# Per-partition running maxima, joined once, in a fused attention and soft-MoE kernel with a written-out order

## The chip, the cores and the metric

The kernel runs on one core of one Trainium2 chip. The time is device microseconds of one execution. Before the change three runs took 286.15, 287.49 and 510.6 us, so the median is 287.49; the third run is far off the other two. The profiled execution took 286.1 us, and its span, from the first to the last instruction, is 284.3 us.

## The reference

Four batches of 5056 tokens with 256 channels go through an attention over channels and then, all 20224 tokens together, through a soft mixture of experts with 32 slots (8 experts with 4 slots each). Cut to what matters:

```python
qn, kn = q / norm(q over tokens), k / norm(k over tokens)
s = kn.T @ qn / tau                    # 256 x 256 for each batch
a = softmax of s over its last axis
x = v @ a                              # tokens x 256, all batches stacked
logits = x @ phi                       # tokens x 32
d = softmax of logits over all tokens  # one column for each slot
slot_input = d.T @ x                   # 32 x 256
slot_out = relu(slot_input @ w1[e]) @ w2[e]      # expert of each slot
c = softmax of logits over the 32 slots          # one row for each token
out = c @ slot_out
```

The softmax over tokens needs for each slot a maximum over the tokens of all batches. Any value that stands for the maximum cancels, as long as sums and weights are scaled by the same one.

## The kernel before

**Tiling.** A batch is cut into ten units of 512 tokens (`UB`, a load `raw` of 1 MB with q and k) and into five pieces of 1024 tokens (`PB`, numbered p = 0 to 19, a load `v` of 1 MB). TensorE adds up S = k.T q over the units (L226), partly from fp32 data (`raw`) and partly from a split into a rounded value and a rest (`hl`, made by ScalarE at L182 and VectorE at L188). ScalarE squares each unit (L203) and VectorE adds the squares (L209) for the norms. After a batch's last unit the steps `att_*` turn S into the attention matrix a and into M = a times phi (L332), which the logits need.

**Logits.** The logits of a piece need v turned, with channels on partitions, in two halves m of 512 KB. A half is either loaded turned from HBM (`vt`; the set `LT` lists these pairs (p, m)) or turned on TensorE (`turn`, L351, eight transposes for a half) and copied by ScalarE (L356). `logits` (L378) leaves a bank of 128 partitions with four blocks of 32 slots: a partition holds one slot for a quarter of the piece's tokens. From this bank ScalarE copies the raw logits (`lt`, L399), VectorE takes a maximum (`mxs`, L405) and transposes 32x32 blocks into `nat` (L409), which has tokens on partitions.

**Groups and the running maximum.** The pieces of a batch form two groups, of three and of two pieces (`GR`). When a group's maxima are there, a chain joins the four blocks and the groups so far: `peak` (L415) on VectorE, `peak_row` (L420, a matmul that lays the 128 maxima in a row), `peak_run` (L426 to L431, maximum over the blocks and over the past), `shift` (L435, a matmul back onto partitions) and `shifted` (L440, L444: the negative maximum `negm` and the step `al` from the one before). Only then can ScalarE take the exponential (L456, in place in `lt`), VectorE transpose it to weights `dn` (L466), and `gather` on TensorE (L485) add weights times v. `finish_*` scale and add up groups and batches: a fold of the four blocks by a matmul with `fold` (L506), and a sum over batches `acc` on 32 partitions (L539). After the last batch come `last_*` (slot inputs, L547 to L575) and the experts (`up`, `relu`, `flip_h`, `back_h`, `down`, L642 to L673), whose weights are loaded into buffers that the loop has left (`load_w1`, `load_w2`).

**Output.** For each batch `c_max` to `c_mul` (L580 to L598) make the softmax over slots in `nat`, `c_flip` (L608) transposes it back, and `out_mul` (L712), `out_evict` (L734, L736) and `store` (L742, L744) write the result. Stores of the first five pieces are split into two halves of columns, because the experts' output comes in two halves.

**Order.** Every step is put in a list with a key, and the list `ORDER` of numbers says in which order the steps are emitted. Each engine runs its own part of this order strictly in sequence, and SyncE issues all DMAs in it, waiting at each for its buffer (5 buffers `raw`, 3 `hl`, 6 `v`, 3 for each `vt` half).

## Time and profile before

| what | value |
|---|---|
| median of the runs shown | 287.49 us |
| profiled execution, its own time | 286.1 us |
| its span | 284.3 us |
| TensorE busy | 248.8 us (88%) |
| VectorE busy | 236.4 us (83%) |
| ScalarE busy | 185.0 us (65%) |
| bytes moved by DMA | 115.61 MB, mean 407 GB/s |
| mean granted TensorE clock | 0.959 |

Busy time of TensorE is that of its matmuls; the loads of their weights (PEld) run beside them. The 40 slices of the page are 7.1 us each. The DMA row shows what share of the time the 16 DMA engines were moving packets, and below it how many bytes they moved. In the queries by stretch of time, each row has the stretch, then busy time and number of instructions of PE, PEld, DVE (VectorE), ACT (ScalarE) and POOL (GpSimd), then the granted clock, the DMA share and GB/s.

### The profile page before, as it was taken

To read this page: it belongs to the slowest core of one execution; us is meant where nothing else is said; L and a number is where in the kernel's file an instruction comes from. 1 tells how busy PE (TensorE), PEld (TensorE's weight loads), DVE (VectorE), ACT (ScalarE), POOL (GpSimd) and SP (SyncE) were. 2 spreads that over 40 slices of the span, in tenths; PEclk is the share of its full clock that TensorE was granted. 3 is DMA by queue.
4 is the path that set the end of the run, shared out by engine and by line. 5 is a ranking of instruction groups with operands and counts; after the bars stand their busy time and mean duration, and the time that the engine had idled before them with its cause. 6 is when DMAs were issued, how large, how long until landed. Compare 5 with 4: busy or idle time off the path is not lost. (4 is left out here: it accounts for less than half of the span.)

```text
span 284.3 us, 6083 instructions
## 1 busy us (share of the span) xinstructions
PE 248.8 (88%) x2448; PEld 201.1 (71%) x2448; DVE 236.4 (83%) x389; ACT 185.0 (65%) x264; POOL 9.8 (3%) x10
## 2 busy tenths in 40 slices
PE   6899999999999999999999999999889898984000
PEld 6699998897898978878778686786553777763000
DVE  1699999899999999999999999988768688994100
ACT  4997897889899796687777957175613436862200
POOL 0000002200003000000200000100000000000000
PEclk9999999999999999999999999999999999998555
DMA  7999999999999999999999999999999998999996
GB/s 280 428 418 420 417 421 424 422 420 414 414 422 368 399 427 422 422 407 422 415 424 421 415 418 422 418 427 417 422 413 414 414 372 323 410 423 418 426 424 260
DMA packets 19900, 115.61 MB, mean 407 GB/s; under 512 B 2336, under 2 KB 2336, under 8 KB 9248
## 3 DMA queue, kind: packets, MB, share of 16 engines
q1 hardware_dynamic: 19872, 115.22, 98.4%
q8 instruction: 19, 0.31, 0.4%
q14 instruction: 9, 0.07, 0.1%
HBM read 94.24 MB, written 20.97 MB: 405 GB/s over the span
## 5 line engine op out<-in xcount | busy, mean ns | idle before, releaser
L209 DVE TENSOR_TENSOR sq<-sq,sq 128x1024 f32<-128x1024 f32 (+1 forms) x63 | 85.2, 1366 | 1.3 <-ACT sq L203 0.6
L203 ACT ACTIVATE sq<-raw 128x2048 f32<-128x2048 f32 x40 | 76.2, 1911 | 15.2 <-DVE sq L209 6.7
L226 PE MATMUL S<-raw 128*128 128x256 f32 x328 | 80.1, 384 | 2.2 <-DMA raw<-in_qk_dram 2.2
L226 PE MATMUL S<-hl 128*128 128x256 f32 x468 | 70.9, 297 | 0.1
L226 PEld LDWEIGHTS S<-raw 128*128 128x128 f32 x328 | 58.8, 190 | 12.7 <-issue 3.3
L226 PEld LDWEIGHTS S<-hl 128*128 128x128 f32 x468 | 61.0, 190 | 3.2 <-issue 1.2
L188 DVE TENSOR_TENSOR hl<-raw,hl 128x1024 fp32r<-128x1024 f32 x39 | 46.8, 1214 | 6.9 <-ACT hl L182 6.9
L182 ACT CAST hl<-raw 128x1024 fp32r<-128x1024 f32 x39 | 40.2, 1041 | 2.6 <-PE S L226 1.7
L736 DVE COPY o<-op_None 128x512 f32<-128x512 f32 x30 | 18.7, 675 | 7.6 <-issue 6.9
L734 ACT COPY o<-op_None 128x512 f32<-128x512 f32 x30 | 15.8, 593 | 12.2 <-issue 7.9
L712 PE MATMUL op_None<-so,cT 32*128 32x256 f32 x240 | 18.6, 401 | 1.9 <-ACT o L734 1.3
L485 PE MATMUL G<-v,dn 128*32 128x256 f32 x320 | 20.1, 382 | 0.1
L712 PEld LDWEIGHTS op_None<-so,cT 32*128 32x128 f32 x240 | 14.6, 184 | 5.6 <-ACT o L734 2.7
L378 PE MATMUL L<-vt,M 128*32 128x256 f32 (+1 forms) x272 | 17.7, 380 | 0.9 <-ACT M L332 0.9
L356 ACT COPY vt<-vTp 128x512 f32<-128x512 f32 x18 | 10.4, 583 | 11.1 <-PE vTp L351 11.1
L248 POOL TENSOR_TENSOR rn<-rn,half 128x4 f32<-128x4 f32 x4 | 9.0, 2262 | 173.4 <-DVE rn L243 173.4
L485 PEld LDWEIGHTS G<-v,dn 128*32 128x32 f32 x320 | 10.0, 109 | 6.6 <-issue 0.5
L351 PE MATMUL vTp<-ident,v 128*128 128x128 f32 x96 | 14.1, 276 | 0.0
L378 PEld LDWEIGHTS L<-vt,M 128*32 128x32 f32 x272 | 8.1, 109 | 6.9 <-ACT M L332 1.3
L351 PEld LDWEIGHTS vTp<-ident,v 128*128 128x128 f32 x96 | 11.1, 143 | 2.4 <-issue 1.2
L399 ACT COPY lt<-L 128x256 f32<-128x256 f32 x20 | 7.2, 372 | 7.6 <-DVE mxs L405 3.4
L734 ACT COPY o<-op 128x256 f32<-128x256 f32 x20 | 6.3, 380 | 7.1 <-PE op L712 7.1
(111 smaller groups left out, 250.2 us busy)
## 6 DMA issues: line engine op xcount, KB each, us to landing
raw<-in_qk_dram SPq DMA_DIRECT2D x40, 1024.0 KB, 8.7
v<-in_v_dram SPq DMA_DIRECT2D x20, 1024.0 KB, 10.0
out_dram<-o SPq DMA_DIRECT2D x15, 1024.0 KB, 12.0
vt<-in_vt_dram SPq DMA_DIRECT2D x21, 512.0 KB, 8.7
w<-in_moe_w_dram SPq DMA_DIRECT2D x8, 1024.0 KB, 13.8
w<-in_moe_w_dram SPq DMA_DIRECT2D x16, 512.0 KB, 10.0
out_dram<-o SPq DMA_DIRECT2D x10, 512.0 KB, 4.3
vt<-in_vt_dram SPq DMA_DIRECT2D x4, 480.0 KB, 9.3
```

The source lines that it names most:

```text
L182: act.copy(hl[:, :ns, 0::2, :], raws[u][:, :ns])
L188: dve.tensor_tensor(hl[:, :ns, 1::2, :], raws[u][:, :ns], hl[:, :ns, 0::2, :].bitcast(F32), op=ALU.subtract)
L203: act.activation(sq, raws[u], AF.Square)
L209: dve.tensor_tensor(a[:, lo:hi], a[:, lo:hi], s[:, lo:hi], op=ALU.add)
L226: pe.matmul(sm, w, x, start=first, stop=False, skip_group_check=True)
L351: pe.transpose(tp[:, P * jj : P * jj + P], vs[p][:, 4 * h + jj, P * m : P * m + P], ident)
L356: act.copy(x[:, h * UT : h * UT + UT], tps[p, h, m])
L378: pe.matmul(L[S * g : S * g + S, :n, :], M[:, m, :], x[:, :n, S * g : S * g + S], start=m == 0, stop=m == 1,)
L485: pe.matmul(gp[S * g : S * g + S, :C], dn[:, x, j, :], vt[:, j, :], start=x == 0 and j < G, stop=x == n - 1 and j >= G,)
L712: pe.matmul(ops[b, p, hf, g][:, h, :], cT[b][S * g : S * g + S, 4 * i : 4 * i + 4, :].rearrange("s j t -> s (j t)"), so[S * g : S * g + S] ...
L734: act.copy(dst, src)
L736: dve.tensor_copy(dst, src)
```

## The change

The running maximum is no longer joined over the four blocks at each group. Each of the 128 partitions keeps its own running (negative) maximum: `logit_max` writes the negative maximum of a piece beside the running one, `peak` takes the minimum of the group's and the running one in a single reduction, and the exponentials use that as their bias. `peak_row`, `peak_run`, `shift` and `shifted` are gone. Since the four blocks of a slot now have maxima of their own, folding them is put off: for the first three batches the fold's matmul is a plain transpose (with `ident`), `acc` has 128 partitions and `gts` 128 columns. After the last group `join_*` makes one factor for each partition (a matmul, a reduction, a product, a reduction, an exponential) and puts it into the last batch's fold (`fw`), into the product that folds `acc` (`fa`) and into the sum `zacc`.

The raw logits are copied into a buffer that stays for the whole batch (`lg`); the exponentials go to a buffer of their own (`el`). `logit_nat` is now one transpose from `lg` for a whole batch, ahead of its `c_max`, and the five transposes from the PSUM banks are gone. `c_flip` writes back into `lg`, in five parts for the first batch and in two (2 and 3 pieces) for the others.

`LT` gets `- {(6, 1), (13, 1)}`. In Python a difference of sets binds more tightly than a union, so the two pairs are taken out of the last set of the expression, `{(10, 1), (13, 1), (15, 1)}`, alone; (6, 1) is still in an earlier one. The list goes from 28 turned loads to 27, and piece 13 gets two more rounds of transposes.

`ORDER` is a new list (974 steps for 1022), and the warm-up has 9 matmuls for 7.

```diff
-WAKE = 7
+WAKE = 9
+NY = 2
-LT = {(p, 0) for p in range(15)} | {(p, 1) for p in range(0, 15, 3)} | {(p, 0) for p in range(15, 20)} | {(10, 1), (13, 1), (15, 1)}
+LT = {(p, 0) for p in range(15)} | {(p, 1) for p in range(0, 15, 3)} | {(p, 0) for p in range(15, 20)} | {(10, 1), (13, 1), (15, 1)} - {(6, 1), (13, 1)}
 ORDER = [
-    1, 0, 2, 5, 3, 4, 13, 7, 8, 9, 10, 23, 6, 14, 16, 15, 31, 606, 18, 22, 17, 19, 25, 24, 21, 27, 36, 32, 41, 12,
+    615, 1, 0, 4, 2, 14, 7, 8, 12, 11, 13, 32, 9, 10, 3, 5, 18, 19, 31, 41, 16, 17, 22, 25, 26, 30, 29, 577, 21, 40,
...
     def logit_max(p):
         b, gi, x, n = group(p)
-        if x == 0:
-            mxs[b, gi] = bpool.tile([P, 3], F32, tag="mxs", name=f"mxs{b}_{gi}", bufs=2)
-        dve.tensor_reduce(mxs[b, gi][:, x : x + 1], Ls[p], axis=AX.XY, op=ALU.max)
+        m = mx_tile(b, gi)
+        dve.tensor_reduce(m[:, x + 1 : x + 2], Ls[p], axis=AX.XY, op=ALU.max, negate=True)
 
-    def logit_nat(p):
-        b, q = divmod(p, PB)
+    def logit_nat(b, q, n):
+        if b not in nat:
+            nat[b] = keep.tile([P, 8 * PB, S], F32, tag="nat", name=f"nat{b}", bufs=NY)
         dve.transpose(
-            nat[b][:, 8 * q : 8 * q + 8, :].rearrange("p j s -> p (j s)"), Ls[p].rearrange("p j s -> p (j s)")
+            nat[b][:, 8 * q : 8 * q + 8 * n, :].rearrange("p j s -> p (j s)"),
+            lg[b][:, q : q + n].rearrange("p q x -> p (q x)"),
         )
...
     def peak(b, gi):
+        m = mx_tile(b, gi)
+        negm = mx_tile(*after(b, gi))[:, 0:1]
+        lo = 1 if (b, gi) == (0, 0) else 0
+        dve.tensor_reduce(negm, m[:, lo : 1 + GR[b][gi]], axis=AX.X, op=ALU.min)
         negms[b, gi] = negm
         if (b, gi) != (0, 0):
             al = bpool.tile([P, 1], F32, tag="al", name=f"al{b}_{gi}", bufs=3)
-            dve.tensor_tensor(al, negm, run["negm"], op=ALU.subtract)
+            dve.tensor_tensor(al, negm, m[:, 0:1], op=ALU.subtract)
             als[b, gi] = al
...
+    def join_row():
+        t = bank(X1, "join")
+        pe.matmul(t[:, :P], negms[B - 1, gl].broadcast_to([P, P]), ident, start=True, stop=True)
+        run["join"] = t
+
+    def join_top():
+        top = bpool.tile([P, S], F32, tag="top", name="top")
+        dve.tensor_reduce(top, run["join"][:, :P].rearrange("p (g s) -> p s g", g=G), axis=AX.X, op=ALU.min)
+        dve.tensor_tensor(top, top, fold, op=ALU.mult)
+        jm = bpool.tile([P, 1], F32, tag="jm", name="jm")
+        dve.tensor_reduce(jm, top, axis=AX.X, op=ALU.add)
+        run["jm"] = jm
+
+    def join_exp():
+        wj = bpool.tile([P, 1], F32, tag="wj", name="wj")
+        act.activation(wj, negms[B - 1, gl], AF.Exp, bias=run["jm"], scale=-1.0)
+        run["wj"] = wj
+
+    def join_fold():
+        run["fw"] = bpool.tile([P, S], F32, tag="fw", name="fw")
+        dve.tensor_scalar_mul(run["fw"], fold, run["wj"])
+
+    def join_acc():
+        run["fa"] = bpool.tile([P, S], F32, tag="fa", name="fa")
+        dve.tensor_scalar_mul(run["fa"], run["fw"], st[B - 1]["be"])
...
-            pe.matmul(slp[d][:, :S], accv[:, d, :], ident[:S, :S], start=True, stop=False)
+            pe.matmul(slp[d][:, :S], accv[:, d, :], run["fa"], start=True, stop=False)
...
-        at(k + 0.43, logit_nat, p)
...
+        tail(ts_[0], logit_nat, b, 0, PB)
...
-            tail(t, c_flip, b, p)
+        tail(t, c_flip, b, 0, 2)
+        tail(t, c_flip, b, 2, 3)
```

What the new list does is seen in the queues. Three places follow.

The first is SyncE's queue near the start, before: the sixth DMA is already a `raw` that waits for a buffer.

```order
L120 DMA raw_86<-in_qk_dram 128x2048
L120 DMA raw_151<-in_qk_dram 128x2048
L120 DMA raw_157<-in_qk_dram 128x2048
L134 DMA vt_1_161<-in_vt_dram 128x1024
L120 DMA raw_171<-in_qk_dram 128x2048
L134 DMA vt_1_229<-in_vt_dram 128x1024
```

The same place after the change, from the fifth `raw` on; `w_2_277` is the second layer of expert 2 (its first half here, its second half six DMAs later).

```order
L117 DMA raw_86<-in_qk_dram 128x2048
L136 DMA few_sb<-in_few_dram 128x67
L125 DMA v_191<-in_v_dram 128x2048
L117 DMA raw_216<-in_qk_dram 128x2048
L117 DMA raw_233<-in_qk_dram 128x2048
L642 DMA w_2_277<-in_moe_w_dram 128x1024
```

A `v` and a weight of the experts have moved ahead; that weight keeps one of the six `v` buffers until the end of the program.

The second place is TensorE's queue at the last batch's two groups, before (`rp` and `cp` are the two matmuls of the chain, `G` the gather, `slp` and `gt` the slot inputs).

```order
L378 MATMUL L_2083<-x_1843,M_2020 32x256 x8
L420 MATMUL rp_0_2094<-ident,mx_0_2079 128x128
L506 MATMUL gt_2098<-fold,gs_1852 128x32 x2
...
L435 MATMUL cp_0_2122<-negone,rowrun 128x1
L420 MATMUL rp_1_2136<-ident,mx_1_2127 128x128
L531 MATMUL sp_2148<-a_1406,gts_2105 32x256 x2
L435 MATMUL cp_1_2151<-negone,rowrun 128x1
L485 MATMUL G_0_2153<-v_1764,dn_0_2145 32x256 x8
```

And after the change, from the last batch's first logits to the gathers.

```order
L372 MATMUL L_1937<-vt_0_1935,M_1920 32x256 x4
L372 MATMUL L_1937<-vt_1_1905,M_1920 32x256 x4
L345 MATMUL vTp_0_1_1948<-ident,v_1770 128x128 x4
L345 MATMUL vTp_1_1_1960<-ident,v_1958 128x128 x4
L345 MATMUL vTp_0_1_1967<-ident,v_1958 128x128 x4
L345 MATMUL vTp_1_1_1973<-ident,v_1808 128x128 x4
...
L517 MATMUL sp_2091<-a_1446,gts_2010 128x256 x2
L531 MATMUL join<-ident,mxs_0_2049 128x128
L471 MATMUL G_1_2104<-v_1770,dn_1_2056 32x256 x8
```

The four chain matmuls are gone from here, one `join` stands between the two groups' gathers, and four rounds of transposes now stand behind the first logits.

The third place is VectorE's queue there, before: the last batch's maxima, its `nat` transposes and the chain.

```order
L405 TENSOR_REDUCE mxs_0_2046<-L_2036 128x1
L409 STREAM_TRANSPOSE nat_113<-L_2027 128x256
L409 STREAM_TRANSPOSE nat_113<-L_2048 128x256
L409 STREAM_TRANSPOSE nat_113<-L_2036 128x256
L405 TENSOR_REDUCE mxs_0_2046<-L_2048 128x1
...
L440 COPY negm_0_2129<-cp_0_2122 128x1
L444 TENSOR_TENSOR al_0_2131<-negm_0_2129,negm_1_1883 128x1
L409 STREAM_TRANSPOSE nat_113<-L_2108 128x256
L426 TENSOR_REDUCE row_1_2138<-rp_1_2136 1x32
```

And after: `lg` rows are flips of batches 0 and 1.

```order
L401 TENSOR_REDUCE mxs_0_1784<-L_1993 128x1
L418 TENSOR_REDUCE mxs_1_2003<-mxs_0_1784 128x1
...
L619 STREAM_TRANSPOSE lg_108<-nat_1090 128x256
L449 STREAM_TRANSPOSE dn_0_2021<-el_0_2015 128x256 x3
L619 STREAM_TRANSPOSE lg_109<-nat_1717 128x512
L401 TENSOR_REDUCE mxs_1_2003<-L_2028 128x1
L401 TENSOR_REDUCE mxs_1_2003<-L_2018 128x1
L418 TENSOR_REDUCE mxs_0_2049<-mxs_1_2003 128x1
```

The three maxima and `peak` now follow each other, and the second group's maxima stand behind the transposes of the first group's weights.

More of the change, by code (lines that the diff above doesn't have):

```diff
@@ L164, in colnorm_attention_soft_moe @@
     fold4 = fold4.rearrange("p g s -> p (g s)")
-    nat = [keep.tile([P, 8 * PB, S], F32, tag="nat", name=f"nat{b}", bufs=B) for b in range(B)]
-    acc = keep.tile([S, C], F32, name="acc")
+    lg = [keep.tile([P, PB, 8 * S], F32, tag="lg", name=f"lg{b}", bufs=B) for b in range(B)]
+    nat = {}
+    acc = keep.tile([P, C], F32, name="acc")
     zacc = keep.tile([P, 1], F32, name="zacc")
-    rowrun = keep.tile([P, G, S], F32, name="rowrun")
-    dve.memset(rowrun, 0.0)
     rz = keep.tile([P, 2], F32, name="rz")
@@ L391, in group, with mx_tile @@
             q -= n
-    lts, mxs, dns, als, negms = {}, {}, {}, {}, {}
+    els, mxs, dns, als, negms = {}, {}, {}, {}, {}
     def logit_copy(p):
-        b, gi, x, n = group(p)
-        if x == 0:
-            lts[b, gi] = bpool.tile([P, 3, 8 * S], F32, tag="lt", name=f"lt{b}_{gi}")
-        act.copy(lts[b, gi][:, x], Ls[p].rearrange("p j s -> p (j s)"))
+        b, q = divmod(p, PB)
+        act.copy(lg[b][:, q], Ls[p].rearrange("p j s -> p (j s)"))
+    def mx_tile(b, gi):
+        if (b, gi) not in mxs:
+            mxs[b, gi] = bpool.tile([P, 4], F32, tag="mxs", name=f"mxs{b}_{gi}", bufs=4)
+        return mxs[b, gi]
@@ L416, in peak @@
-        st[b]["mx", gi] = mx
-    def peak_row(b, gi):
-        rp = bank(X1, f"rp{b}_{gi}")
-        pe.matmul(rp[:, :P], st[b]["mx", gi].broadcast_to([P, P]), ident, start=True, stop=True)
-        st[b]["rp", gi] = rp
-    def peak_run(b, gi):
-        rp = st[b]["rp", gi]
-        row = bpool.tile([1, 1, S], F32, tag="row", name=f"row{b}_{gi}", bufs=2)
-        dve.tensor_reduce(row[:, 0, :], rp[0:1, :P].rearrange("p (g s) -> p s g", g=G), axis=AX.X, op=ALU.max)
-        row4 = row.broadcast_to([1, G, S])
-        if (b, gi) == (0, 0):
-            dve.tensor_copy(rowrun[0:1], row4)
-        else:
-            dve.tensor_tensor(rowrun[0:1], rowrun[0:1], row4, op=ALU.max)
@@ L433, in shift @@
-    def shift(b, gi):
-        cp = bank(X1, f"cp{b}_{gi}")
-        pe.matmul(cp[:, 0:1], rowrun.rearrange("p g s -> p (g s)"), negone, start=True, stop=True)
-        st[b]["cp", gi] = cp
-    def shifted(b, gi):
-        negm = bpool.tile([P, 1], F32, tag="negm", name=f"negm{b}_{gi}", bufs=3)
-        dve.tensor_copy(negm, st[b]["cp", gi][:, 0:1])
+        m = mx_tile(b, gi)
+        negm = mx_tile(*after(b, gi))[:, 0:1]
+        lo = 1 if (b, gi) == (0, 0) else 0
+        dve.tensor_reduce(negm, m[:, lo : 1 + GR[b][gi]], axis=AX.X, op=ALU.min)
@@ L443, in shifted @@
             al = bpool.tile([P, 1], F32, tag="al", name=f"al{b}_{gi}", bufs=3)
-            dve.tensor_tensor(al, negm, run["negm"], op=ALU.subtract)
+            dve.tensor_tensor(al, negm, m[:, 0:1], op=ALU.subtract)
             als[b, gi] = al
-        run["negm"] = negm
     zs_ = {}
@@ L503, in finish_fold @@
         gs = st[b]["gs"]
-        gt = bank(X0, f"gt{b}")[:, : 2 * S].rearrange("p (m s) -> p m s", m=2)
+        w = P if b < B - 1 else S
+        gt = bank(X0, f"gt{b}")[:, : 2 * w].rearrange("p (m s) -> p m s", m=2)
         for m in range(2):
-            pe.matmul(gt[:, m, :], gs[:, P * m : P * m + P], fold, start=True, stop=True)
+            pe.matmul(gt[:, m, :], gs[:, P * m : P * m + P], ident if b < B - 1 else run["fw"], start=True, stop=True)
         st[b]["gt"] = gt
     def finish_mul(b):
-        gts = bpool.tile([P, 2, S], F32, tag="gts", name=f"gts{b}")
+        w = P if b < B - 1 else S
+        gts = bpool.tile([P, 2, P], F32, tag="gts", name=f"gts{b}")[:, :, :w]
         for m in range(2):
@@ L530, in finish_slots @@
         for m in range(2):
-            pe.matmul(sp_[:S, :C], gts[:, m, :], a[:, m, :], start=m == 0, stop=m == 1)
+            pe.matmul(sp_[:, :C], gts[:, m, :], a[:, m, :], start=m == 0, stop=m == 1)
         st[b]["sp"] = sp_
@@ L984, in colnorm_attention_soft_moe @@
     for p in range(PB):
-        tail(30.9, c_flip, 0, p)
-    for b, t in ((1, 38.0), (2, 44.5), (3, 49.5)):
-        for p in range(PB):
-            tail(t, c_flip, b, p)
+        tail(10.0, c_flip, 0, p, 1)
+    for b, t in ((1, 17.6), (2, 31.3), (3, 49.5)):
+        tail(t, c_flip, b, 0, 2)
+        tail(t, c_flip, b, 2, 3)
     NHF = 5
```

74 lines of the change are left out of this document (36 added, 38 removed), and 86 rows, old and new, of the table ORDER.

## The prediction

> **What bounds the kernel now.** I read the page's shares and slices first, then stretches of time, then SyncE's waits, then the order of time at the end.
>
> From the page: engines, DMA share and GB/s in 40 slices, and bytes.
>
> ```profile
> PE 248.8 (88%) x2448; PEld 201.1 (71%) x2448; DVE 236.4 (83%) x389; ACT 185.0 (65%) x264; POOL 9.8 (3%) x10
> ...
> DMA  7999999999999999999999999999999998999996
> GB/s 280 428 418 420 417 421 424 422 420 414 414 422 368 399 427 422 422 407 422 415 424 421 415 418 422 418 427 417 422 413 414 414 372 323 410 423 418 426 424 260
> DMA packets 19900, 115.61 MB, mean 407 GB/s; under 512 B 2336, under 2 KB 2336, under 8 KB 9248
> ```
>
> DMA is full in nearly every slice and moves about 420 GB/s there. So the time is bytes over rate plus the places where the rate drops: the ends, slices 13 and 14, and slices 33 and 34. Stretches of 7 us show these places (PE, PEld, DVE, ACT, POOL busy, clock, DMA share, GB/s).
>
> ```profile
> 28.00:35.00 7.00, 7.00 (x46) 6.41 (x46) 6.90 (x5) 5.64 (x5) 0.00 (x0) 1.00 1.02 416
> 84.00:91.00 7.00, 7.00 (x54) 6.17 (x58) 6.83 (x12) 6.41 (x7) 3.00 (x1) 1.00 0.97 381
> 91.00:98.00 7.00, 7.00 (x55) 6.22 (x48) 6.97 (x13) 5.46 (x9) 0.00 (x0) 1.00 0.99 389
> 175.00:182.00 7.00, 6.97 (x86) 4.63 (x84) 7.00 (x11) 2.44 (x5) 0.00 (x0) 1.00 1.00 410
> 224.00:231.00 7.00, 6.00 (x152) 4.59 (x143) 5.57 (x13) 2.21 (x8) 0.00 (x0) 1.00 1.00 397
> 231.00:238.00 7.00, 6.24 (x174) 5.42 (x165) 4.84 (x14) 3.21 (x13) 0.00 (x0) 1.00 0.78 307
> 238.00:245.00 7.00, 6.19 (x97) 5.41 (x98) 6.43 (x14) 5.51 (x13) 0.00 (x0) 1.00 1.01 396
> 259.00:266.00 7.00, 0.34 (x3) 0.00 (x0) 0.40 (x1) 0.00 (x0) 0.00 (x0) 0.65 1.03 430
> ```
>
> Against 420 GB/s the stretch 84 to 98 loses (39 + 31) x 7 / 420 = 1.2 us, and 224 to 245 loses (23 + 113 + 24) x 7 / 420 = 2.7 us. The second hole is where the loads have run out and the stores have not begun in earnest. In the loop TensorE and VectorE are as full as DMA, so three resources run level there.
>
> What SyncE waits for tells who keeps the next load back.
>
> ```profile
> SPq L120 <- PE S L226: 54.5, 23, 6.2
> SPq L128 <- PE G L485: 13.0, 7, 3.9
> ```
>
> The first hole follows such a wait: SyncE's order of time shows two `raw` loads in one row, the second issued 8 us after the first at 79.80; SyncE stood some 7.7 us between them, while what was in flight ran out.
>
> ```profile
> 79.80 8.04 SPq L120 DMA_DIRECT2D raw<-in_qk_dram  x2
> ```
>
> The end of the program is a chain from the last batch's norms to the first store (the columns are start, length, what, and in brackets the idle time before it).
>
> ```profile
> 187.84 0.59 PE L270 MATMUL rq<-dg,ones 128*128 128x256 f32 x2
> 191.73 1.04 PE L351 MATMUL vTp<-ident,v 128*128 128x128 f32 x8
> 194.07 1.07 PE L378 MATMUL L<-vt,M 128*32 128x256 f32 x16 [0.43 <-ACT M L332]
> 198.82 0.49 PE L420 MATMUL rp<-ident,mx 128*128 128x128 f32 x2
> 201.31 0.38 PE L435 MATMUL cp<-negone,rowrun 128*128 128x1 f32 x2
> 207.35 1.93 PE L485 MATMUL G<-v,dn 128*32 128x256 f32 x32
> 209.96 0.63 PE L506 MATMUL gt<-fold,gs 128*128 128x32 f32 x4 [0.67 <-DVE gs L500]
> 211.99 5.36 PE L642 MATMUL H<-w,slT 128*32 128x512 f32 x48
> 202.23 0.51 ACT L456 ACTIVATE lt<-lt,negm 128x256 f32<-128x256 f32 x1 [1.94 <-DVE negm L440]
> 204.75 0.65 ACT L399 COPY lt<-L 128x256 f32<-128x256 f32 x2 [0.85 <-DVE negm L440]
> 227.91 12.28 SPq L744 DMA_DIRECT2D out_dram<-o  x9
> ```
>
> Stores cannot begin before this chain is through, whatever the loads gain. A change therefore shows in the time by the smaller of two shifts: that of the first store, and what DMA can give back (holes and bytes).
>
> **The change part by part.** The rows that price it, by line and form:
>
> ```profile
> L351 PE MATMUL vTp<-ident,v 128*128 128x128 f32 x96 | 14.1, 276 | 0.0
> L420 PE MATMUL rp<-ident,mx 128*128 128x128 f32 x16 | 3.5, 299 | 0.5 <-DVE negm L440 0.5
> L435 PE MATMUL cp<-negone,rowrun 128*128 128x1 f32 x16 | 2.6, 230 | 0.1
> L426 DVE TENSOR_REDUCE row<-rp 1x32 f32<-1x128 f32 x8 | 2.1, 260 | 0.0
> L431 DVE TENSOR_TENSOR rowrun<-rowrun,row 1x128 f32<-1x128 f32 x7 | 2.0, 279 | 0.2
> L440 DVE COPY negm<-cp 128x1 f32<-128x1 f32 x8 | 1.1, 141 | 0.1
> L409 DVE STREAM_TRANSPOSE nat<-L 128x256 f32<-128x256 f32 x20 | 8.5, 434 | 0.1
> L466 DVE STREAM_TRANSPOSE dn<-lt 128x768 f32<-128x768 f32 x3 | 2.9, 958 | 0.0
> L466 DVE STREAM_TRANSPOSE dn<-lt 128x512 f32<-128x512 f32 x3 | 2.1, 706 | 1.0 <-ACT lt L456 1.0
> L583 DVE TENSOR_TENSOR nat<-nat,cm 128x1280 f32<-128x1280 f32 x4 | 5.9, 1475 | 0.0
> L460 ACT ACTIVATE al<-al 128x1 f32<-128x1 f32 x7 | 1.4, 199 | 0.0
> vt<-in_vt_dram SPq DMA_DIRECT2D x21, 512.0 KB, 8.7
> ```
>
> *Bytes.* The set expression takes only (13, 1) out, so one load of 512 KB goes: 0.524 MB / 420 GB/s = 1.25 us of DMA. Two would have been 2.5 us; the queue of the changed kernel has 27 turned loads, so this is settled. In return piece 13 has two more rounds of four transposes.
>
> *TensorE in the loop.* Ahead of the last batch's `rq` stand 6 `rp` and 6 `cp`, two instructions each, 24 in all. In a burst TensorE does 8 transposes in 1.04 us (191.73), 0.13 each; so they cost 24 x 0.13 = 3.1 us, and the added 8 transposes 1.0 us: 2.1 us less ahead of `rq`. By their busy rows it would be 6/8 of (3.5 + 2.6) less 8 x 0.147, 3.4 us; if another resource sets the pace, 0. I take 2.1, since TensorE is at 7.00 of 7.
>
> *VectorE in the loop.* Ahead of the fourth batch's norms 14 transposes from PSUM (14 x 0.434 = 6.1 us) become one of 128x1280, for which 706 and 958 ns at 512 and 768 columns give 252 ns for each 256 more, so an estimated 1.46 us. Five times `row`, `rowrun` and `negm` (0.68 us together) are 3.4 us. That is 8 us less before the change moves three of the passes over whole batches behind this point too. It takes VectorE out of the first place, but TensorE and DMA keep theirs, so I count nothing for it beyond letting the first hole close in part.
>
> *The chain at the end.* ScalarE stood 1.94 and 0.85 us for `negm`, 2.8 us in all; after the change the exponentials wait for `peak` alone. In exchange come the join (a matmul as `cp`, 0.23 us, then a reduction, a product, a reduction, an exponential and a product, five small steps of 0.14 to 0.26 us by the rows of `negm`, `row` and `al`). It runs beside the second group's gather (1.93 us), so I count half of its estimated 1.2 us on the path; and the second group's maxima now stand behind the first group's third `dn` transpose (about 0.4 us). Net 2.8 - 0.6 - 0.4 = 1.8 us. Bounds: nothing gained, or a loss of 1.2 us, if the join is wholly on the path and VectorE's queue takes the gain; 4.0 us if the five `nat` transposes among the last batch's steps (5 x 0.434 = 2.2 us of VectorE) were on it and the join is not seen.
>
> *The rest.* A wider `acc` and `gts` are the same rows of 128 partitions with other widths, within 0.1 us each. `c_flip` into `lg` and `nat` with two buffers wait for `out_mul` or for an earlier batch; both lie beside DMA's backlog after 245 us, which covers them. If the last two batches' softmax came late there, each of its passes (1.475 us) would cost less than a store's time (1.05 MB at the 430 GB/s of 259 to 266, 2.44 us). The warm-up matmuls lie ahead of the first load.
>
> *The queue in front.* `few`, a `v` and half an expert weight are issued before the sixth `raw`, which covers VectorE's slow start; but the weight holds a `v` buffer for good (below).
>
> Sum: the first store moves by 2.1 + 1.8 = 3.9 us. DMA can give back 1.25 + 1.2 + 2.7 = 5.1 us, which is more, so the chain decides: 286.1 (the profiled execution's own time, 1.8 over its span) - 3.9 = 282.2 us. The median of the runs shown, 287.49, is the slower of its two undisturbed runs and 0.5% over the profiled one; my sum keeps to the profiled one.
>
> **The rivals.**
>
> *DMA alone sets the end.* If TensorE has headroom in the loop, VectorE's 8 us and the 1.8 of the end shift the first store by more than 5.1 us, and all holes close: 286.1 - 5.1 = 281.0 us; with every slice but the first and last at 423 GB/s some 279.3. For it: PEld is busy only 4.6 to 6.4 of 7 us in the loop. Against it: SyncE's longest sum of waits is for `S` on TensorE, 54.5 us. [...]
>
> *The gain turns into another wait.* In place of `negm` the chain waits for VectorE's queue: the second group's maxima behind `dn`, then the join's five steps, then `fw` before the fold. The end gains nothing and the loop's 2.1 us are lost in order-made gaps: a shift of 0 to 1, about 285.6 us. For it: in the trace TensorE's gaps in the chain are short, 0.43 us at 194.07 and 0.67 at 209.96, so there is no large stall to remove.
>
> *Slower: five `v` buffers.* From its load near the start one expert weight keeps one of six buffers, so each `v` load waits for a gather that comes one piece later, and behind it in SyncE's queue stand the `raw` loads. The trace has 7 such waits, the longest 3.9 us, without a hole; a stand of 7.7 us gave 1.2 us of hole. If all seven pass about 6 us, 7 x 1.2 = 8.4 us come in: 286.1 - 1.25 + 8.4 = 293.3 us. Against it: the new list has fewer loads ahead of some `raw` and VectorE is emptier.
>
> **How the numbers follow.** Forecast 282.2 us, chance 0.44; DMA alone (281.0) 0.27; another wait (285.6) 0.20; slower (293.3) 0.09. The range 279.3 to 287.0 takes in the first three with their bounds. I take 2% as what a measurement of this kernel tells from no change; against the median it is 281.7, so rival one counts as faster, with a small part of the forecast: 0.30. Slower by 2% is the last rival alone, 0.09; within 2% stays 0.61.
>
> **What would show it.** Right: 115.1 MB; the last batch's first logits near 192 instead of 194.07; no wait of ScalarE over 1 us before its last exponentials; first store near 224; the stretch around it over 380 GB/s in place of 307. Wrong: the first store where it was (rival two), or a new stretch under 380 GB/s in the loop behind a wait of SyncE for a gather (rival three). If the loop's row `S` ends 5 us earlier, rival one.

## The result, and the profile after

The changed kernel takes 289.58 us in the median of 20 runs, the kernel before 287.52 on the same chip: 1.0079 times as long, 95% interval 1.0054 to 1.0103. That is within 2%, and on the slow side, with the interval clear of 1. The profiled execution took 287.81 us, with a span of 286.0. The forecast was 282.2 us, with a range of 279.3 to 287.0, and failed: the time lies above the range.

From the page of the kernel after, the same rows as of before: engines, granted clock, DMA share and GB/s in 40 slices, bytes.

```profile
PE 255.8 (89%) x2430; PEld 205.9 (72%) x2430; DVE 234.7 (82%) x343; ACT 187.5 (66%) x267; POOL 8.5 (3%) x10
...
PEclk9999999999999999999999999999999999796555
DMA  7999999999999999999999999999999989999697
GB/s 286 427 417 416 416 426 418 422 409 416 419 419 400 407 414 405 418 413 420 416 408 420 406 411 424 408 419 420 417 408 408 408 336 385 418 415 379 276 411 329
DMA packets 19755, 115.08 MB, mean 402 GB/s; under 512 B 2320, under 2 KB 2320, under 8 KB 9104
```

The bytes are those of the forecast, 115.1 MB. The holes at slices 13 and 14 (368, 399 before) are shallower, those at 33 and 34 (372, 323 before) are a little smaller together. But there is a new hole at slices 37 and 38, 379 and 276 GB/s, where before had 418 and 426. The same in stretches of 7 us (PE, PEld, DVE, ACT, POOL busy, clock, DMA share, GB/s):

```profile
84.00:91.00 7.00, 7.00 (x59) 5.77 (x58) 6.26 (x8) 5.87 (x7) 0.32 (x1) 1.00 1.01 411
91.00:98.00 7.00, 7.00 (x49) 6.58 (x48) 6.87 (x12) 5.93 (x8) 1.54 (x1) 1.00 1.01 399
224.00:231.00 7.00, 6.04 (x138) 4.80 (x139) 4.33 (x11) 2.85 (x9) 0.00 (x0) 1.00 0.97 383
231.00:238.00 7.00, 6.18 (x155) 5.47 (x155) 6.59 (x18) 3.09 (x11) 0.00 (x0) 1.00 0.86 342
238.00:245.00 7.00, 3.87 (x59) 3.07 (x51) 6.76 (x11) 4.42 (x9) 0.00 (x0) 1.00 0.99 403
245.00:252.00 7.00, 6.10 (x74) 5.11 (x77) 6.37 (x11) 3.48 (x7) 0.00 (x0) 0.76 1.02 415
252.00:259.00 7.00, 5.46 (x67) 4.10 (x64) 4.66 (x9) 3.98 (x9) 0.00 (x0) 1.00 1.01 419
259.00:266.00 7.00, 5.91 (x32) 3.59 (x36) 2.95 (x5) 2.64 (x5) 0.00 (x0) 0.50 0.87 352
266.00:273.00 7.00, 4.78 (x30) 2.99 (x30) 2.87 (x5) 2.24 (x4) 0.00 (x0) 0.50 0.72 297
```

Against 420 GB/s the stretches 259 to 273 lose (68 + 123) x 7 / 420 = 3.2 us. There TensorE still multiplies, at a granted clock of 0.50; before it had 0.34 us of work left after 259. The products of whole output tiles cost more per piece and wait for the flips (before first, after second):

```profile
L712 PE MATMUL op_None<-so,cT 32*128 32x256 f32 x240 | 18.6, 401 | 1.9 <-ACT o L734 1.3
```

```profile
L723 PE MATMUL op_None<-so,lg 32*128 32x256 f32 x240 | 26.2, 491 | 7.8 <-DVE lg L619 3.9
```

The chain from the last batch's norms to the first product of the output, in order of time (start, length, what, idle time before it):

```profile
186.32 0.59 PE L264 MATMUL rq<-dg,ones 128*128 128x256 f32 x2
192.56 1.07 PE L372 MATMUL L<-vt,M 128*32 128x256 f32 x16
198.43 0.37 ACT L391 COPY lg<-L 128x256 f32<-128x256 f32 x1 [1.77 <-DVE mxs L401]
202.40 0.70 ACT L391 COPY lg<-L 128x256 f32<-128x256 f32 x2 [1.41 <-DVE mxs L401]
205.97 0.29 ACT L544 ACTIVATE wj<-mxs,jm 128x1 f32<-128x1 f32 x1 [1.53 <-DVE jm L539]
209.71 5.36 PE L653 MATMUL H<-w,slT 128*32 128x512 f32 x48
221.18 0.42 PE L684 MATMUL O<-w,hT 128*32 128x128 f32 x6 [0.34 <-DVE hT L675]
221.90 1.94 PE L684 MATMUL O<-w,hT 128*32 128x128 f32 x58 [0.30 <-DMA w<-in_moe_w_dram]
225.06 0.94 PE L723 MATMUL op<-so,lg 32*128 32x128 f32 x20 [0.35 <-ACT so L705]
```

The norms' row is 1.5 us earlier than before (187.84), the first layer 2.3 us (211.99), the first product 1.2 us (226.28). The first store goes out at 226.68 instead of 227.91. So there are two questions: what happens after 253 us, and why no more than 1.2 us reach the first store.

### The profile page after: what moved, and what is told of

It is laid out like the page before. It is cut to its first block, busy times and chain, and to the rows that moved or that the text cites. A ratio compares the mean times of both kernels' runs of the same rounds, so it can differ in the third digit from the quotient of the medians.

```text
span 286.0 us, 5995 instructions
## 1 busy us (share of the span) xinstructions
PE 255.8 (89%) x2430; PEld 205.9 (72%) x2430; DVE 234.7 (82%) x343; ACT 187.5 (66%) x267; POOL 8.5 (3%) x10
## 2 busy tenths in 40 slices
DMA packets 19755, 115.08 MB, mean 402 GB/s; under 512 B 2320, under 2 KB 2320, under 8 KB 9104
## 5 line engine op out<-in xcount | busy, mean ns | idle before, releaser
L723 PE MATMUL op_None<-so,lg 32*128 32x256 f32 x240 | 26.2, 491 | 7.8 <-DVE lg L619 3.9
L723 PEld LDWEIGHTS op_None<-so,lg 32*128 32x128 f32 x240 | 18.7, 234 | 14.3 <-issue 5.6
L471 PE MATMUL G<-v,dn 128*32 128x256 f32 x320 | 18.9, 381 | 0.0
L372 PE MATMUL L<-vt,M 128*32 128x256 f32 x272 | 17.5, 382 | 0.1
L345 PE MATMUL vTp<-ident,v 128*128 128x128 f32 x104 | 15.6, 277 | 0.3 <-ACT x L350 0.2
L350 ACT COPY vt<-vTp 128x512 f32<-128x512 f32 x20 | 11.6, 580 | 5.8 <-PE vTp L345 5.7
L471 PEld LDWEIGHTS G<-v,dn 128*32 128x32 f32 x320 | 10.8, 110 | 6.0 <-DVE dn L449 0.4
L391 ACT COPY lg<-L 128x256 f32<-128x256 f32 x20 | 7.2, 372 | 11.3 <-DVE mxs L401 8.1
L345 PEld LDWEIGHTS vTp<-ident,v 128*128 128x128 f32 x104 | 12.0, 142 | 3.5 <-issue 1.2
L242 POOL TENSOR_TENSOR rn<-rn,half 128x4 f32<-128x4 f32 x4 | 7.8, 1945 | 169.2 <-DVE rn L237 169.2
```

What stands on the lines that cost most here:

```text
L345: pe.transpose(tp[:, P * jj : P * jj + P], vs[p][:, 4 * h + jj, P * m : P * m + P], ident)
L350: act.copy(x[:, h * UT : h * UT + UT], tps[p, h, m])
L372: pe.matmul(L[S * g : S * g + S, :n, :], M[:, m, :], x[:, :n, S * g : S * g + S], start=m == 0, stop=m == 1,)
L471: pe.matmul(gp[S * g : S * g + S, :C], dn[:, x, j, :], vt[:, j, :], start=x == 0 and j < G, stop=x == n - 1 and j >= G,)
L723: pe.matmul(ops[b, p, hf, g][:, h, :], cT[b][S * g : S * g + S, 4 * i : 4 * i + 4, :].rearrange("s j t -> s (j t)"), so[S * g : S * g + S] ...
```

## Experiments

**The late stores.** When the last eviction of an output tile ended and when its store was issued, from the trace of after (us; y is a second half):

```
block_tile  evicted  issued  landed
0_2y        238.37   274.29  285.02
1_2         251.81   270.72  278.78
2_1         256.97   271.69  281.26
1_0         254.32   254.38  263.11
0_0y        259.28   259.34  264.73
1_3         262.13   262.19  267.20
2_2         265.64   265.70  269.58
3_2         269.80   269.87  273.75
3_3         269.21   270.29  276.39
3_0         273.31   273.37  283.73
```

Three finished stores, 0.52 + 1.05 + 1.05 MB or 6.1 us of DMA time, stand in SyncE's queue behind stores that are not ready, while DMA runs dry. And the last tiles become ready 3.0 us apart (six products from 253.82 to 271.93), with a store of 1 MB taking 2.44 (at the 430 GB/s of before, 259 to 266 us). Three runs separate the two. The first moves the three stores alone:

(`...` marks lines left out, here and below.)

```diff
 store 0_1y
+store 0_2y
 store 1_4
...
 store 2_4
+store 1_2
 store 2_0
 store 1_0
+store 2_1
 store 0_0y
...
 store 3_3
-store 1_2
-store 2_1
 store 3_0
-store 0_2y
```

> After, with three stores moved on SyncE's queue to the place right behind the last eviction of their tile: the second half of block 0 of tile 2 (ready at 238.37 us, issued at 274.29), block 1 tile 2 (251.81, issued 270.72) and block 2 tile 1 (256.97, issued 271.69). No other engine's order changes. Theory Q (the finished stores stand behind unfinished ones on an in-order queue while the DMA engines run dry from 259 to 273 us): the 6.1 us of stores fill the holes of 3.2 us (rates of 352 and 297 GB/s in 259:266 and 266:273 become 400 and more), the last store still is issued near 273 and the end comes 2.5 to 3.5 us earlier, a time 0.988 to 0.992 of after, 0.995 to 1.000 of before. Theory P (the late output products on TensorE alone set the end): the last product is as late as it was, 271 us, its store lands 10 us later as in after, and the time stays within 0.5 us of after, 1.006 to 1.010 of before. A third view, that the end is set by the loads' slower packets: no change of more than 0.5 us either.

Measured: 286.76 us, 0.9987 of before (0.9960 to 1.0015). The profile shows the holes filled while the products are as late as in after:

```profile
259.00:266.00 7.00, 5.62 (x28) 3.34 (x28) 3.23 (x6) 2.64 (x5) 0.00 (x0) 0.54 1.01 417
266.00:273.00 7.00, 5.07 (x31) 3.22 (x30) 2.64 (x5) 2.25 (x4) 0.00 (x0) 0.50 1.01 419
```

The second leaves the stores in their order and makes the products faster. `out_mul` takes its four PSUM banks by the tile's number in the plan; the new order takes 2_1 and 3_2, and then 1_3, 2_2 and 3_3, from the same four. The edit alternates the banks in the order of execution and puts a tile's evictions together (in after two of 3_2's evictions stand behind the product of 3_3):

```diff
     def out_mul(b, p, hf, k):
         ring = rings[hf]
+        if hf != 0:
+            k = run["k"] = run.get("k", 5) + 1
```

> After, with the last six output tiles double-buffered again: their PSUM banks alternate in the order in which TensorE takes the tiles (in after the tiles 3_2; 1_3, 2_2, 3_3 and 3_0 follow each other partly on the same four banks), and the four evictions of a tile stand together behind its product. The stores keep their order, the three held ones at the end. Theory P (products and evictions take turns on the same banks, so each of the last six tiles takes 3 us against 2.44 us for its store): the last product ends 5 us or more earlier (before 268 us), all stores are issued by 268 us, the two holes of 259 to 273 us are gone, time 2.5 to 3.5 us less than after, 0.995 to 1.000 of before. Theory Q alone (order on SyncE's queue): the stores in question still wait behind block 3 tile 3, so not over 1.5 us less. If instead the granted clock (0.50 from 259 us) sets the pace of the products, the tiles still take 2.5 to 3 us each, with less gain, 0 to 1.5 us.

Measured: 287.03 us, 0.9989 of before (0.9962 to 1.0016). TensorE's order of time from 254 us on, in this run and then in after:

```profile
255.62 2.64 PE L725 MATMUL op_None<-so,lg 32*128 32x256 f32 x32
258.56 5.25 PE L725 MATMUL op_None<-so,lg 32*128 32x256 f32 x64 [0.30 <-ACT o L747]
```

```profile
253.82 1.78 PE L723 MATMUL op_None<-so,lg 32*128 32x256 f32 x16
256.77 1.91 PE L723 MATMUL op_None<-so,lg 32*128 32x256 f32 x22 [1.17 <-ACT o L745]
259.33 2.07 PE L723 MATMUL op_None<-so,lg 32*128 32x256 f32 x10 [0.65 <-DVE o L747]
261.81 2.44 PE L723 MATMUL op_None<-so,lg 32*128 32x256 f32 x16 [0.41 <-ACT o L745]
264.60 4.11 PE L723 MATMUL op_None<-so,lg 32*128 32x256 f32 x22 [0.35 <-ACT o L745]
269.86 2.07 PE L723 MATMUL op_None<-so,lg 32*128 32x256 f32 x10 [1.14 <-DVE o L747]
```

Four tiles (64 instructions) take 5.25 us in one piece, where after needed about 3 us for each of its last six, with waits for evictions between. The granted clock keeps 1.00 through 259 to 266 us here; in after it fell to 0.50 behind those waits and made each product longer still (22 matmuls of one form took 1.91 us from 256.77 on, at 1.00, and 4.11 us from 264.60 on, at 0.50). So the half clock came from the shared banks and the divided evictions, which this edit changes together; no run tells the two apart.

> The two edits of the runs before together. If both theories name the same 3.2 us of dry DMA engines, the gain is not the sum: 2.5 to 3.7 us less than after, no more than 0.7 us below the better of the two alone, about 0.995 of before. If the products were also holding back other stores (the first hole, 224 to 245 us, is not touched), nothing of that is seen here: 224:231 and 231:238 stay near 383 and 342 GB/s. A gain of 5 us or more would say that there is a second loss at the end that I have not seen.

Both edits together: 286.87 us, 0.9986 (0.9964 to 1.0009). By the ratios to the kernel before, either edit gives back about 2.6 us (from 1.0079 to 0.9987 or 0.9989) and the second adds nothing to the first, so they repair one and the same hole. It takes both faults to open it.

**The loads.** With the end repaired the kernel stands where it was before, not 3.9 us under it. The loads tell a part of the reason. In the built programs the tiles of `v` and the turned `v` begin at a multiple of 256 bytes in a partition before, and 224 bytes past one after, since constants and small tiles ahead of them have changed; `raw` begins 224 bytes past one before and 64 after. The first run is a control.

> The kernel before, unchanged, profiled beside the three runs that follow, as a control for the loads. In the two profiles the last load lands at 230.70 us (before) and 230.94 us (after), although after moves 0.5 MB less (1.25 us at 420 GB/s) and its gap in the loads at 84 to 98 us is gone. If the slower packets of after (1.26 us per 512 KB against 1.23 us) belong to the chip of that day, this run shows 1.25 to 1.26 us for the old kernel too and a last load at about 232 to 234 us. If they belong to the new order, it shows 1.23 us and a last load within 0.5 us of 230.70.

It took 286.71 us in its one run. The last load of the old kernel landed at 232.09 us in this second profile, 1.4 us later than in the first, while its transfers took the same time (1.239 us per 512 KB). So the slower packets are not the chip's, but the last load is not where that expectation had it. One profile's last landing can't carry a term of 1.25 us. What does carry is the sum of the gaps between landings, split into transfers and holes. Of the next four runs, three only add unused tiles, with sizes that differ, and no instruction changes; e6_after_all adds them to the kernel with both repairs. In e4_align and e5_shift the tiles are these:

```diff
+    const.tile([P, 8], F32, name="pad0")
     ones = const.tile([P, P], F32, name="ones")
...
+    bpool.tile([P, 56], F32, name="pad1")
     raws, sqs = {}, {}
```

> After, with an unused tile of 32 bytes per partition among the constants and one of 224 bytes among the small tiles: the loaded tiles of `v` and of the turned `v` begin at a multiple of 256 bytes in a partition, as they do in the kernel before (in after they begin 224 bytes past one); the `raw` tiles stay 64 bytes past one as in after. Nothing else is edited, the late stores of after included. Theory A (a transfer into a tile that does not begin at a multiple of 256 bytes takes 1.6 to 2.4% longer): the median gap between landings goes from 2.49 to 2.45 us for `v` and from 1.26 to 1.23 us for the turned loads, `raw` stays at 2.49; 17 `v` x 0.04 + 24 turned x 0.03 + 6 weights x 0.04 = 1.6 us, the last load lands near 229.5 us in place of 230.94 to 232.65, and the time is 1.0 to 1.8 us less than after. Theory O (the order of the loads, or what the engines do beside them, makes the packets slower): the gaps stay at 2.49 and 1.26 us and the time stays within 0.5 us of after, 1.006 to 1.010 of before.

> The kernel before with the same two unused tiles: its `v` and turned tiles now begin 32 bytes past a multiple of 256 bytes, its `raw` tiles stay 224 bytes past one. Theory A: the gap of `v` goes from 2.45 to 2.49 us, that of the turned loads from 1.23 to 1.26 us, the last load lands 1.3 to 1.8 us later, time 1.004 to 1.007 of before. Theory O: no gap changes, time 0.998 to 1.002 of before.

> After with the three held stores moved, the alternating banks and the joined evictions of the runs above, and with `v`, turned and `raw` tiles all at multiples of 256 bytes. Theory A: the gap of `raw` goes from 2.49 to 2.45 us too, 40 x 0.04 = 1.6 us beside the 1.6 us of the run above, so the loads end 3 us earlier than in the runs with the same stores (231.0 to 232.7), near 228.5, and if TensorE and the chain at the end allow the stores to follow, the time is 2.5 to 3.5 us less than the 286.9 us of those, 0.987 to 0.991 of before. If the first store is then bound by the chain of TensorE instead of by the second layer's weights (they landed at 221.86 us, the product on them ended 223.84), 1.0 to 2.0 us of it are lost in the hole at 224 to 245 us: 0.991 to 0.995 of before. Theory O: 0.998, as without the padding.

> The kernel before with one unused tile of 32 bytes among the small tiles, which puts its `raw` tiles at a multiple of 256 bytes too (its `v` and turned tiles are at one already). Theory A: the gap of `raw` 2.45 us in place of 2.49, the last load 1.3 to 1.6 us earlier; as TensorE's chain ends at the same place and its first store comes when it came, the time gains 0 to 1.6 us, 0.994 to 1.000 of before. Theory O: the gap stays at 2.49 us, 0.998 to 1.002.

Worked out from the landings of each trace between 31 us and the last load (bytes past a multiple of 256; transfer time per 512 KB; the transfer of a load is the median gap of the loads of its size in the same trace, and holes are what a gap has over it, from 0.17 us up; the runs named here and not yet above follow below):

```
kernel         v, turned  raw   us/512 KB  holes us  last load us
before               0    224      1.239      3.5      230.70
b0_before            0    224      1.239      4.2      232.09
e5_shift            32    224      1.254      2.2      231.81
e7_before_all        0      0      1.229      4.9      230.78
after              224     64      1.255      2.5      230.94
e1_stores          224     64      1.255      2.5      231.02
e2_banks           224     64      1.254      4.1      232.65
e3_both            224     64      1.257      3.0      231.79
e12_off            224     64      1.254      3.4      231.95
e4_align             0     64      1.238      5.5      231.07
e6_after_all         0      0      1.225      6.6      229.98
e8_warm              0      0      1.224      6.9      230.50
e13_on               0      0      1.227      6.2      229.95
e9_load              0      0      1.226      7.8      232.87
e11_w2_late          0      0      1.229      8.6      232.63
```

The expectations of e9_load, e11_w2_late and e13_on below give e6_after_all 5.1 or 5.2 us of holes; with the size that the trace has for each load, among them a weight of 512 KB that landed 0.9 us late, it is 6.6.

By kind the median gap is 2.49 against 2.45 us for `v` and `raw` and 1.26 against 1.23 for turned loads, in each kernel by the place of the tile, in the old order as in the new. Theory O falls. In time the padded kernels gave: e4_align 1.0072 (1.0038 to 1.0105), no gain, since its end still had the hole, and a deeper one (329 and 256 GB/s at 259 to 273 us); e5_shift 1.0024 (0.9994 to 1.0055), less than expected and not clear of none; e6_after_all 0.9947 (0.9915 to 0.9979); e7_before_all 0.9978 (0.9937 to 1.0019), not clear of none either. Where transfers got shorter, holes grew (from e3_both to e6_after_all 1.257 to 1.225 us per 512 KB, and 3.0 to 6.6 us of holes). Two more runs put the repaired kernel with and without the padding side by side.

> After with the three stores moved, alternating banks and joined evictions; loaded tiles where after has them (224 and 64 bytes past a multiple of 256). It is timed beside the next run on one chip, since the two were only compared through the kernel before so far (0.9986 and 0.9947, with intervals that overlap). If the place of the tiles is worth time, this one is 0.6 to 1.5 us slower than the next; if TensorE's pace takes all of it back, the two are within 0.4 us.

> The same with all loaded tiles at multiples of 256 bytes. Transfer time from 31 us to the last load by the landings: 1.224 us per 512 KB here against 1.250 in the run beside it, 157 to 158 such units, 4.1 us of transfer less; the holes between landings 5.2 against 3.3 us, so 2.2 us should be left at the last load and 0.6 to 1.5 us in the time, since the first stores wait for TensorE's chain. If nothing is left, the loop is TensorE's alone.

Measured: 286.90 us without, 285.86 with it, 0.9967 (0.9936 to 0.9997) and 0.9923 (0.9887 to 0.9958) of before. The transfers are 196.4 - 192.3 = 4.1 us shorter, the holes 2.8 us longer, the last load 2.0 us earlier (0.7 us of that lies ahead of 31 us), the time 1.04 us less. So the place of the tiles is worth about a microsecond, and the rest of it goes to what the loads wait for. This kernel (e6_after_all and e13_on are the same) is 0.5 and 0.8% faster than before in its two runs, both intervals clear of 1 though under the 2% that the prediction asked for; the kernel after was not timed beside it.

**What the loads wait for.** SyncE's waits before, and after:

```profile
SPq L120 <- PE S L226: 54.5, 23, 6.2
SPq L120 <- DVE hl L188: 31.8, 17, 5.3
```

```profile
SPq L117 <- DVE hl L182: 60.1, 24, 6.5
SPq L117 <- PE S L220: 29.7, 20, 3.9
```

86.3 us in two rows before, 89.8 after: what `raw` loads no longer wait for on TensorE they now wait for on VectorE, although VectorE is 4.0 us less busy from 14 to 224 us (before, then after). Which part of the new order makes it so, no run shows.

```profile
14.00:224.00 210.00, 206.49 (x1844) 166.91 (x1846) 198.72 (x313) 153.20 (x205) 9.05 (x4) 1.00 1.01 417
```

```profile
14.00:224.00 210.00, 205.96 (x1849) 167.37 (x1847) 194.70 (x272) 155.45 (x208) 7.78 (x4) 1.00 1.01 415
```

Two runs ask for the worth of single loads, both from the kernel of e6_after_all:

```diff
-LT = ... | {(10, 1), (13, 1), (15, 1)} - {(6, 1), (13, 1)}
+LT = ... | {(10, 1), (13, 1), (15, 1)}
```

> The same kernel without the extra matmuls, with the turned load of `v` tile 13's second half put back (the one the change dropped): 8 transposes of TensorE (8 x 0.13 = 1.0 us) and two evictions of ScalarE less, 0.5 MB (1.23 us) more to load. Theory T (with faster packets the loop's pace is TensorE's, and the DMA engines stand idle 5.1 us in it): the last batch's first logits come 0.5 to 1.0 us earlier, the load disappears in the gaps, time 0.3 to 1.0 us less, 0.991 to 0.994 of before. Theory D (bytes set the end, as the prediction's 1.25 us for this load had it): 0.9 to 1.3 us more, 0.998 to 0.999 of before.

286.94 us, 0.9979 (0.9944 to 1.0014) of before, 1.1 us more than e8_warm, timed beside it, e6_after_all and e13_on (285.85, 285.86 and 285.86). With six runs whose times lie 3 us apart this favours theory D, that the load which the change dropped is worth what its bytes take, by little more than the noise. In the profile the norms' row is 1.4 us later than e6_after_all's (188.37) and the first layer 3.3 us (213.79); between them the granted clock was 0.50 from 195.1 to 198.5 us, so the 3.3 us are not the load's alone.

```diff
 load_qk 5
-load_w2 2, 0
 load_qk 6
...
-load_w2 2, 1
 load_qk 15
...
 load_w2 1, 0
+load_w2 2, 0
...
 load_w2 1, 1
+load_w2 2, 1
```

> The kernel with moved stores, alternating banks and all loaded tiles at multiples of 256 bytes, with the two early loads of the second layer's weights of expert 2 (issued among the first loads of the loop, where they hold one of the six v buffers to the end) moved behind those of expert 1. Six v buffers then stand free for v in the loop. With the early loads the profile of this kernel has 5.2 us of holes between landings from 31 to 230 us, four of them ahead of a v or turned load. Theory V (the missing buffer makes the loads wait, the prediction's third rival): the holes shrink by 1.5 to 3 us, the last load lands 1 to 2 us earlier than 229.98 and the time is 0.5 to 1.5 us less, 0.989 to 0.993 of before. Theory T (TensorE's pace frees the buffers, and 1 MB loaded early is 1 MB less at the end): the holes stay within 1 us, what is loaded later lands later, time the same or up to 1 us more, 0.994 to 0.999 of before.

286.69 us, 0.9985 (0.9963 to 1.0007). The holes did not shrink with six buffers for `v`, they grew to 8.6 us, 1.6 of them at the weights' loads after 220 us, the last load lands 2.7 us later and the time is 0.8 us more, on another chip. Theory V and the prediction's third rival fall; the outcome is theory T's. What the early weight gains is not shown: up to 35 us e6_after_all and this run move about the same, 13.8 and 13.9 MB.

**The clock ahead of the first layer.** In some profiles of the new order, with the padding and without, the first layer's 48 products take 6.9 us instead of 5.36. From e6_after_all, which has it, and then from e3_both, which has not, the stretch in question:

```profile
206.80:210.20 3.40, 2.85 (x30) 2.25 (x22) 1.98 (x11) 0.44 (x3) 0.00 (x0) 1.00 1.01 422
210.20:213.60 3.40, 3.40 (x19) 0.99 (x22) 3.30 (x7) 0.18 (x1) 0.00 (x0) 0.50 1.01 416
```

```profile
206.80:210.20 3.40, 2.85 (x30) 2.40 (x26) 2.21 (x12) 0.20 (x1) 0.00 (x0) 1.00 1.00 412
210.20:213.60 3.40, 3.40 (x33) 0.99 (x34) 3.33 (x4) 0.19 (x1) 0.00 (x0) 1.00 1.01 411
```

TensorE was as busy from 206.8 to 210.2 us in both, 2.85 of 3.4 us. One run fills the gaps ahead of the first layer with two more matmuls.

```diff
 join_z
+wake(2, T1)
 last_z
```

> The kernel with moved stores, alternating banks and all loaded tiles at multiples of 256 bytes, with two extra matmuls of ones (128x128, 0.24 us each) on TensorE just ahead of the sum over the maxima's tallies, where its trace shows gaps of 0.45 us before the first layer. In that trace the granted clock falls to 0.50 from 210.2 to 213.6 us and the first layer's 48 products take 6.91 us against 5.36 in the profile of after; the fast executions of that kernel lie in two groups, clock 0.959 to 0.965 at 284.8 to 285.9 us and 0.953 to 0.955 at 285.8 to 287.0. Theory C (the gaps ahead of the first layer let the clock drop): the second group goes, the first layer takes 5.4 us, the median is 0.4 to 1.0 us less, 0.991 to 0.993 of before. Rival: the dip comes from somewhere else, both groups stay, 0.994 to 0.996.

285.85 us, 0.9935 (0.9902 to 0.9968), with the dip still in the profile (clock 0.60 and 0.55 from 210 to 214 us) and both groups still there (0.960 to 0.964 at 284.1 and 285.0 us, 0.954 at 285.7 to 286.8). The rival stands: these gaps are not the cause. The groups say less than they seem to: e11_w2_late's profile has the dip and a mean clock of 0.959, because its half clock at the end began 3 us later (268.4 us) than in e6_after_all, e8_warm and e12_off, which have a dip too (264.8 to 265.4 us, 0.953 and 0.954). None of the four profiles of the old order, all of its upper group (0.958 to 0.962), has a dip before 261 us; whether its slower executions have one is not on record.

The traces tell more when the stretches are laid where the clock has them. In all of them the changes of the granted clock lie 3.413 us or a multiple of it apart (in after at 245.32, 248.73 and 258.97 us, 3.413 and 10.240 apart), on a grid that begins elsewhere in each execution: 206.8 to 210.2 us is a stretch of e6_after_all's grid, but e3_both's stretches begin at 204.8 and 208.2. Weigh each matmul's columns by the share of the 128x128 array that it fills (a quarter for `128*32`), and add up what starts in a stretch. Ahead of the dip the sum is 770 to 1538 in the five profiles that have it (e4_align, e6_after_all, e8_warm, e11_w2_late, e12_off). In the five without (after, e1_stores, e2_banks, e3_both, e13_on) the emptier of the last two stretches up to the first layer's start has 1602 to 2370. In e8_warm the two extra matmuls raised the sum from 770 to 1282 only, though TensorE was busy for 0.97 of that stretch. Over all 16 traces, up to 275 us, no half clock follows a stretch with more than 1538, and of the 1168 stretches that full clock follows five have less than 1536. So it is a matter of where the grid falls: in some executions the small products ahead of the first layer get a stretch to themselves. That is read from the traces, no run moves the grid.

**The computation without the new order.**

```diff
-    peak_row, peak_run, shift, shifted, logit_nat(p)
+    logit_nat(b, 0, 5) ahead of c_max(b); c_flip(0), c_flip(1) behind c_mul; join at the last shift
```

> The new computation (maxima per partition, join at the end, raw logits turned per batch, that one load dropped) in the old order: every step that both kernels have stands where it stood before; the turns of a batch stand just ahead of its maxima, the flips of batches 0 and 1 right behind their weights, the join where the last shift stood. Loaded `v` and turned tiles lie at multiples of 256 bytes and `raw` tiles 224 bytes past one, as before. The old order has its stores and banks in turn. If the computation itself is worth what the prediction said (TensorE 2.1 us ahead of the last batch, ScalarE's 2.8 us of waits gone, less 1.0 for the join): last batch's first logits near 192, first layer near 209 instead of 212.0, time 2 to 4 us less, 0.986 to 0.993 of before. If its gain needs the new order: first layer at 211 to 212.5, 0.996 to 1.004. If the flips that now stand early on VectorE hold the chain up: first layer after 212.5, slower than before, 1.003 to 1.010.

1.0232 of before (1.0186 to 1.0277), 292.1 to 295.4 us: the third outcome, and more of it. Up to the third batch's norms nothing differs (139.7 us against 140.0), then the passes over whole batches stand on VectorE ahead of what the loop needs:

```profile
166.82 1.48 DVE L615 TENSOR_TENSOR nat<-nat,cs 128x1280 f32<-128x1280 f32 x1
168.34 1.75 DVE L621 STREAM_TRANSPOSE lg<-nat 128x256 f32<-128x256 f32 x5
197.77 1.49 DVE L408 STREAM_TRANSPOSE nat<-lg 128x1280 f32<-128x1280 f32 x1
199.29 1.49 DVE L597 TENSOR_REDUCE cm<-nat 128x40 f32<-128x1280 f32 x1
200.81 1.49 DVE L600 TENSOR_TENSOR nat<-nat,cm 128x1280 f32<-128x1280 f32 x1
202.22 1.08 DVE L403 TENSOR_REDUCE mxs<-L 128x1 f32<-128x256 f32 x3
```

The first layer starts at 221.75 us instead of 212.0. That overstates it: the profiled execution took 297.76 us, and its granted clock was 0.50 from 205.0 to 215.2 us. The two-buffered `nat` forces the flips that early, so this says that the computation needs an order of its own, not that it costs 2% as such; that the early passes are the cause is read from the order of time, and no run moves them.

## Why the prediction was wrong

By its own steps, with the profiles of before and after:

- *Bytes, -1.25 us.* Right in itself: 115.08 MB, and the load put back costs 1.1 us (e9_load, little more than its noise). But the step took the rate as unchanged. It went from 1.239 to 1.255 us per 512 KB, times 157 makes 2.5 us more, twice the term. The last load lands at 230.94 instead of 230.70 (232.09 in the second profile of before).
- *The first hole, -1.2 us.* It closed (411 and 399 GB/s), but smaller ones opened elsewhere; over the loop the holes are 3.5 and 4.2 us in two profiles of before, and 2.5 to 4.1 in the five unpadded profiles of the new loop. In these profiles such holes are not fixed to a place.
- *TensorE in the loop, -2.1 us.* Mis-sized: 1.5 us at the norms' row in this profile, 0.1 to 1.5 in the five profiles with this loop and these places. The wait for `S` did fall, to 29.7 us; one for `hl` on VectorE took its place.
- *VectorE, counted as nothing.* Right in that no time came of it. Of the 8 us less, 4 remain once the passes that moved ahead are in, and SyncE now waits 60.1 us for it, more than before.
- *The chain at the end, -1.8 us.* Mis-sized: from the norms' row to the first layer 24.15 us became 23.39, 0.8 us. ScalarE no longer waits for `negm`, but 1.77 and 1.41 us for VectorE's maxima of the same tiles, and 1.53 in the join. Half of rival two came true here. Then 1.1 us were lost between the first layer and the first product, which no step had: 0.34 us for a copy on VectorE, 0.30 us for a weight that landed at 221.86, and 0.4 us in the second layer's 128 products, which took 4.29 us in three pieces (1.93, 0.42 and 1.94) where before needed 3.88 in two. TensorE had come early to loads that had not.
- *The first store, 3.9 us earlier.* It was 1.2 us earlier, and in the other profiles of this loop between 1.1 us earlier and 0.6 later. The repaired kernel's 0.5 us in the median (e1_stores, 286.76 against 287.29, an interval that takes in none) answers to that. And the hole around the first stores, of which 2.7 us were to come back, kept 2.2 us.
- *The rest, covered by DMA's backlog after 245 us.* This is the step that failed and made the kernel slower. It priced each late pass by its own length, 1.475 us, against a store's 2.44 us. It did not ask in which order the stores stand in SyncE's queue, nor on which banks the products follow each other. The backlog was there in the form of three finished stores that could not be issued: 3.2 us of holes, and 2.6 us of the time by e1_stores. With the 2.7 us by which the first store came less early than forecast that makes 5.9 us, and the profiled execution missed the forecast by 287.81 - 282.2 = 5.6.

Of the rivals, DMA alone is out: in e13_on transfers 4.1 us shorter left 2.8 us of new holes. Rival three is not what e11_w2_late shows. Of the signs, the bytes and the first logits (192.56 us) came as said; ScalarE's waits, the first store (224) and the rate at 231 to 238 (342, not over 380) did not.

## What to carry to other kernels

A backlog covers a late step only if the queue can issue it (here three finished stores stood behind unfinished ones, with 3.2 us of holes): after a change of order, list for every transfer when its data were ready and when it was issued, and look for finished ones behind unfinished ones. When an order of execution changes, look at whatever was assigned by the old numbering, here PSUM banks by the tile's number, since products and evictions that took turns on two sets of banks can end up on one, though every instruction is still the same. And when tiles of another size are added ahead of the loaded ones, look at where the loaded ones now begin before taking the old rate for the new kernel (here 1.255 us per 512 KB where it had been 1.239).

## What the runs showed of the hardware

In the medians of these traces a load whose tile begins at a multiple of 256 bytes in a partition took 2.45 us per 1 MB (`v` in before, `raw` in e6_after_all), one that begins 32, 64 or 224 bytes past one 2.49 us (`v` at 32 in e5_shift and at 224 in after, `raw` at 64 in after and at 224 in before). For turned loads with rows of 4 KB, 512 KB each, it was 1.23 us (before) and, 224 or 32 bytes past one, 1.26 us (after, e5_shift). The measured cost is 1.6% for rows of 8 KB at each of these distances; what causes it, no run shows.

The granted clock fell to 0.50 for one stretch of 3.413 us (210.2 to 213.6 in e6_after_all) at the first layer in five of the eleven profiles of the new order, and its 48 products took 1.5 to 1.7 us longer there (6.91 us in e6_after_all, 5.36 in after). It did so behind a stretch with little work in the array (770 to 1538 by the measure above), also where TensorE was busy for 0.97 of it.
